# One of the last four units by Strassen's scheme instead of two, and a reordered start of the value loads

## The chip, the core and the metric

The kernel runs on one core of a Trainium2 chip. A core has TensorE (PE; its weight loads are shown apart as PEld), VectorE (DVE), ScalarE (ACT), GpSimd (POOL) and SyncE (SP), each with its own in-order stream of instructions, and 16 DMA engines that all queues share. The metric is the device time of one execution in microseconds (us); lower is better.

## The reference

Two stages. The first is attention over 8 batches of 8 heads with head dimension 64: 32 global and 512 local tokens per batch. Global queries see all 544 keys; a local query sees the 32 global keys and the local keys within 32 positions of its own.

```python
s_g = scale * np.matmul(q_g, k_all.transpose(0, 1, 3, 2))
out_g = np.matmul(sm(s_g), v_all)
s_ll = np.where(np.abs(pos[:, None] - pos[None, :]) <= window, s_ll, -1000000000.0)
a_l = sm(np.concatenate([s_lg, s_ll], axis=-1))
out_l = np.matmul(a_l, np.concatenate([v_g, v_l], axis=2))
```

The second is a mixture of 8 experts over the 4352 resulting rows x (512 wide, 1024 hidden) in which every expert is applied to every row; the weights P come from eight rounds of row and column normalisation.

```python
P = np.exp(logits - logits.max())
for _ in range(8):
    P /= P.sum(1, keepdims=True) + 1e-09
    P /= P.sum(0, keepdims=True) + 1e-09
    P *= N / E
for e in range(E):
    out += P[:, e:e + 1] * (np.maximum(x @ w1[e], 0.0) @ w2[e])
```

The output is 4352 x 512 in float32.

## The kernel before

**Order.** The instructions of each engine run in the order in which the program issues them (`manual_schedule`), so the order of the source is the order of each queue. The framework adds the semaphore waits: an instruction waits for earlier ones that touch the same region of a tile. What it takes for the same region matters here. Partitions are told apart exactly. Columns that interleave are not always: in the program of the kernel before, the first load into `va` (columns 0 to 63 of each 65) waits for the VectorE memset of the ones column (column 64 of each 65, L293), the load into `vb` waits for the memset of its ones column (L294), and the first `vgz` load waits for the POOL copy into the ones column of `vgz` (L298), though none of these pairs shares an element.

**Start.** Before the attention loop the kernel loads the first queries and keys, clears tiles and loads batch 0's values. Loads that change the type to float16 go through POOL's queue (`nc.gpsimd.dma_start`), where issuing one keeps POOL busy for 0.6 to 0.9 us; loads without a change of type go through SP or ACT.

- `steps[2:4]` load queries and keys of heads 4 to 7 of batch 0 (`qs`, `ks`, L174).
- `load_v(b)` returns the steps that load a batch's local values: `first` (L193, with the cast of the global values ahead of it, L183, by `cast_vg`), `mid` (L196, three loads) fill `va`; `last` (L200) fills a part of `vb`; `part` copies the rest of `vb` out of `va`, shifted by half a block of 128 tokens (L204 to L209, for batches 0 and 1 on POOL). 65 columns per head: 64 values and a one, so that the softmax sum comes out of the same matmul.
- `cast_vg(b)` writes the global values of a batch as float16 to a scratch in DRAM (`vg16`); `load_vz(b)` loads them from there into `vgz`, a tile of zeros with the values on a quarter of the partitions for each of four blocks (L180, four loads on SP).
- `clear(i, eng)` sets the first 32 partitions of `va` to zero (L292) and the ones columns of `va` (L293) and `vb` (L294). `clear_z(i, eng)` zeroes `vgz` (L297), writes its ones column (L298) and prepares `vgn` (L300, L301), the global values for the global queries.

**Attention loop.** Each step `s` of 34 works on one pair of heads: `st_A` transposes keys and queries (L332), `st_B` makes scores, maxima and exponentials (L368 to L382), `st_D1` and `st_D2` transpose the probabilities (L389, L399, L403), `st_E` multiplies them with the values (L423: for each block first `va` or `vb`, then `vgz`) and normalises (L427, L428). POOL's queue in step 1 is: four loads of batch 1's queries and keys, the five `vb` copies (`part`), the loads of w1 of expert 0 and of the gate; in step 2 the loads of batch 1's values. `st_E(0)` stands at the end of step 2, and PE's later work queues behind it. From step 5 on matmuls of experts 0 and 1 fill PE's idle time.

**Experts 2 to 7** run as matmuls of quarters by Strassen's scheme (Winograd's form): a `Slot` is a block of the first layer (L969), a `Unit` a block of 256 tokens of the second (L871). A unit needs four sums on its inputs (`sums`, L867) and seven products `m1` to `m7` of four matmuls of 256 columns each; they gather in one tile `z` of PSUM (two buffers) with two ACT copies inside PSUM (L885, L892), and DVE adds them to the output in `r2`, `r7` and `r1` (L905).

**The last four units** `u0` to `u3` have no slot work beside them. `plain(u, last, between)` makes a unit without the scheme: 2 x 8 matmuls of 512 columns (L940) and an addition per half (L943); `between` places other products behind a given matmul. Before: `u0` plain, `u1` and `u2` by the scheme, `u3` plain with the rest of `u2` in between; the sums of `u2` run on POOL, those of `u1` on DVE. With `last`, the second half is cut in columns of 256, 128 and 128.

Of the kernel before, what the change touches and what calls it, by code (L numbers as in the profile page):

```python
# [23 lines left out]
def kernel(  # L24
# [13 lines left out]
    nc = tc.nc  # L38
# [14 lines left out]
    FT = F // P  # L53
# [75 lines left out]
    with ExitStack() as att:  # L129
# [13 lines left out]
        vgr = [att_c.tile([P, 4 * H * VW], FP16, name=f"vgz{i}") for i in range(2)]  # L143
# [8 lines left out]
        def natural(b):  # L152
            return b < 2
# [18 lines left out]
        def load_qk(b, *hs):  # L172
            staged[b] = tuple(att_in.tile([P, H, NJ, Dh], FP16, tag=t, name=t) for t in ("qs", "ks"))
            return [lambda t=t, src=src, h0=h0, h1=h1: nc.gpsimd.dma_start(  # L174
                        out=t[:, h0:h1], in_=src[b, h0:h1].rearrange("h (p s) d -> p h s d", s=NJ))
                    for h0, h1 in zip(hs, hs[1:]) for t, src in zip(staged[b], (q_l, k_l))]

        def load_vz(b):
            for i in range(4):
                nc.sync.dma_start(out=vgz[b % 2][i:P:4, i, :, 0:Dh], in_=vg16[b])  # L180

        def cast_vg(b):
            nc.gpsimd.dma_start(out=vg16[b], in_=v_g[b].rearrange("h g d -> g h d"))  # L183

        def load_v(b):
            va, vb = vab[b % 2]
            vz = vgz[b % 2]
            src = v_l[b].rearrange("h s d -> s h d")

            def first():  # L190
                if b != 1:
                    cast_vg(b)
                nc.gpsimd.dma_start(out=va[W:P, 0, :, 0:Dh], in_=src[0:96])  # L193

            def mid(j):
                nc.gpsimd.dma_start(out=va[:, j, :, 0:Dh], in_=src[P * j - W : P * j + 96])  # L196

            def last():
                r = HB if natural(b) else W
                nc.gpsimd.dma_start(out=vb[r : r + W, NJ - 1, :, 0:Dh], in_=src[Sl - W : Sl])  # L200

            def part(eng, lo):
                if lo:
                    eng.tensor_copy(out=vb[96:P, NJ - 1], in_=va[W : 2 * W, 0])  # L204
                    eng.tensor_copy(out=vb[0:HB, 0:2], in_=va[HB:P, 0:2])
                    eng.tensor_copy(out=vb[0:HB, 2:NJ], in_=va[HB:P, 2:NJ])
                else:
                    eng.tensor_copy(out=vb[HB:P, 0:2], in_=va[0:HB, 1:3])
                    eng.tensor_copy(out=vb[HB:P, 2], in_=va[0:HB, 3])  # L209

            def move():
                if natural(b):
                    return part
                nc.sync.dma_start(out=vb[96:P, NJ - 1], in_=va[W : 2 * W, 0])
                nc.sync.dma_start(out=vb[0:W, :], in_=va[HB : HB + W, :])
                nc.sync.dma_start(out=vb[HB : HB + W, :], in_=va[HB + W : P, :])
                nc.sync.dma_start(out=vb[W:HB, 0 : NJ - 1], in_=va[0:W, 1:NJ])
                nc.sync.dma_start(out=vb[HB + W : P, 0 : NJ - 1], in_=va[W:HB, 1:NJ])
                load_vz(b)

            return [first] + [lambda j=j: mid(j) for j in range(1, NJ)] + [last, move]
# [38 lines left out]
        def run(steps):  # L260
            for f in steps:
                f()
# [14 lines left out]
        steps = load_qk(0, 2, 4, H)  # L277
# [12 lines left out]
        def clear(i, eng):  # L290
            va, vb = vab[i]
            eng.memset(va[0:W, 0], 0.0)  # L292
            eng.memset(va[:, :, :, Dh:VW], 1.0)  # L293
            eng.memset(vb[:, :, :, Dh:VW], 1.0)  # L294

        def clear_z(i, eng):
            eng.memset(vgr[i].bitcast(mybir.dt.uint32), 0)  # L297
            eng.tensor_copy(out=vgz[i][:, :, :, Dh], in_=own.unsqueeze(2).to_broadcast([P, 4, H]))  # L298
            if i == 0:
                eng.memset(vgn[0 : P - Sg], 0.0)  # L300
                eng.memset(vgn[P - Sg : P, :, Dh:VW], 1.0)  # L301

        clear(0, nc.vector)
        clear(1, nc.vector)
        for t in range(2):
            (nc.vector.tensor_copy if t else nc.scalar.copy)(out=staged[0][t][:, 0:2], in_=fh[t])
        for a in range(2):
            band = mask[HB * a : HB * (a + 1), 1, 0:KW]
            for base, m, c in ((0, -1, 1), (2 * W, 1, -1)):
                nc.gpsimd.affine_select(out=band, in_=band, compare_op=ALU.is_ge, fill=NEG, base=base,  # L310
                                        pattern=[[c, KW]], channel_multiplier=m)
        run(steps[2:4])
        *steps, move = load_v(0)
        part = move()
        run(steps)
        cast_vg(1)
        clear_z(0, nc.gpsimd)
        load_vz(0)
        nc.sync.dma_start(out=vgn[P - Sg : P, :, 0:Dh], in_=vg16[0])

        st = {}
# [248 lines left out]
        for s in range(NU + 2):  # L570
            b, hp = divmod(s, HP)
# [189 lines left out]
    with tc.tile_pool(name="tpool", bufs=2) as tpool, \  # L761
# [68 lines left out]
        def store(m, c, eng):  # L830
            if m < B:
                r0 = S * m + Sg + P * c
                eng.dma_start(out=out[r0 : r0 + P, :], in_=ogs[m][:, c, :])
            else:
                for b in range(4 * c, 4 * c + 4):
                    eng.dma_start(out=out[S * b : S * b + Sg, :], in_=ogs[m][W * (b % 4) : W * (b % 4 + 1), c, :])
# [15 lines left out]
        class Unit:  # L852
# [6 lines left out]
            def o(self, j):  # L859
                return acc_of(self.m)[:, self.c[j], :]  # L860

            def sums(self, eng=nc.vector):
                a11, a12, a21, a22 = self.a
                s = self.s = hsum.tile([P, 3, HF, P], FP16, tag="hs", name="hs")
                for o, x, y, op in ((s[:, 1], a11, a21, ALU.subtract), (a21, a21, a22, ALU.add),
                                    (s[:, 0], a21, a11, ALU.subtract), (s[:, 2], a12, s[:, 0], ALU.subtract)):
                    eng.tensor_tensor(out=o, in0=x, in1=y, op=op)  # L867

            def mm(self, o, lhs, rhs, first):
                for fk in range(HF):  # L870
# [3 lines left out]
            def w(self, i, j):  # L874
                return w2s[self.k][:, HF * i : HF * (i + 1), H2 * j : H2 * (j + 1)]
# [55 lines left out]
        def plain(u, last, between):  # L931
            order = sorted(range(FT), key=lambda fk: (fk % HF == HF - 1, fk))
            for j in range(2):
                for d0, d1 in ((0, H2), (H2, 3 * P), (3 * P, D)) if last and j else ((0, D),):
                    pool, tag = (ps_sc, "sc") if (j + (d0 > 0)) % 2 else (ps_mm, "mm")
                    z = pool.tile([P, D], FP32, tag=tag, name="zp")
                    for n, fk in enumerate(order):
                        for f in between.get((j, n), ()) if d0 == 0 else ():
                            f()
                        nc.tensor.matmul(z[:, d0:d1], u.a[2 * j + fk // HF][:, fk % HF, :], work["last"][:, fk, d0:d1],  # L940
                                         start=(n == 0), stop=(n == FT - 1), skip_group_check=True)
                    o = u.o(j)[:, d0:d1]
                    nc.vector.scalar_tensor_tensor(out=o, in0=z[:, d0:d1], scalar=u.p[j], in1=o, op0=ALU.mult, op1=ALU.add)  # L943
                store(u.m, u.c[j], nc.sync)
# [171 lines left out]
        p, x = state["slot"], state["unit"]  # L1116
        for w in (x.m4, x.m5, x.r2, x.r7, p.m4, p.m3):
            w()
        u0, u1, u2, u3 = final
        u1.sums()  # L1120
        plain(u0, False, {(0, FT - 2): (x.m3, x.r1, lambda: u2.sums(nc.gpsimd)), (1, 3): (u1.m1,)})
        for w in (u1.m7, u1.m2, u1.m6, u2.m1, u1.m4, u1.m5, u1.r2, u1.r7, u2.m7, u2.m2, u2.m6, u1.m3, u1.r1):
            w()
        plain(u3, True, {(0, 3): (u2.m4, u2.m5, u2.r2, u2.r7), (0, FT - 2): (u2.m3, u2.r1)})


# [28 lines left out]
```

## Time and profile before

| | |
|---|---|
| median of three runs | 996.98 us (996.26 to 997.41) |
| the profiled execution | 996.39 us, of which the span from the first to the last instruction is 994.6 |
| PE busy | 978.8 us, 98% of the span |
| DVE, ACT, POOL busy | 776.9, 659.8, 305.2 us |
| mean granted TensorE clock | 0.998 |

The profile shows one execution; times are in us from the start of the span. A chain of waits is followed back from the last instruction: at each step to what released it, or to the instruction before it on its engine. In a row of a timeline the first two numbers are start and length, `xN` is a number of merged instructions, and the bracket gives the idle time of the engine ahead of it and what ended it. For DMAs the row shows the issue; landing is told apart, in us from the issue.

### The profile page before, as it was taken

To read this page: it belongs to the slowest core of one execution; us is meant where nothing else is said; L and a number is where in the kernel's file an instruction comes from. 1 tells how busy PE (TensorE), PEld (TensorE's weight loads), DVE (VectorE), ACT (ScalarE), POOL (GpSimd) and SP (SyncE) were. 2 spreads that over 40 slices of the span, in tenths; PEclk is the share of its full clock that TensorE was granted. 3 is DMA by queue.
4 is the path that set the end of the run, shared out by engine and by line. 5 is a ranking of instruction groups with operands and counts; after the bars stand their busy time and mean duration, and the time that the engine had idled before them with its cause. 6 is when DMAs were issued, how large, how long until landed. Compare 5 with 4: busy or idle time off the path is not lost.

```text
span 994.6 us, 22109 instructions
## 1 busy us (share of the span) xinstructions
PE 978.8 (98%) x8644; PEld 637.0 (64%) x8644; DVE 776.9 (78%) x1919; ACT 659.8 (66%) x1372; POOL 305.2 (31%) x366
## 2 busy tenths in 40 slices
PE   7899999999999999999999999999999999999997
PEld 5565556555555556666666666676767676766765
DVE  7876666666663755899999888997899999888887
ACT  6898888888884566765555555557765555555551
POOL 9649887887860201111111111101111111100001
PEclk9999999999999999999999999999999999999999
DMA  9999999999952477554443333575654543123043
GB/s 165 189 163 207 226 213 212 224 203 234 225 141 85 121 229 189 161 138 118 117 106 75 75 74 75 138 212 138 160 138 118 117 116 71 38 56 73 2 106 128
DMA packets 138248, 138.65 MB, mean 139 GB/s; under 512 B 56800, under 2 KB 110240, under 8 KB 136096
## 3 DMA queue, kind: packets, MB, share of 16 engines
q0 software_dynamic: 105696, 87.32, 51.6%
q1 hardware_dynamic: 31888, 49.60, 15.7%
q8 instruction: 67, 1.10, 0.4%
q10 hardware_dynamic: 560, 0.33, 0.1%
q14 instruction: 37, 0.30, 0.1%
HBM read 144.46 MB, written 39.58 MB: 185 GB/s over the span
## 4 chain that ended last, share of the span: by engine, by line
PE 93%; DVE 2%; ACT 2%; POOL 1%; DMA 1%; issue 1%; SPq 0%; ACTq 0%; DVEq 0%; POOLq 0%
PE z L871 30%; PE pa L969 18%; PE py L537 12%; PE ph L523 11%; PE pb L969 9%; PE pc L969 4%; PE sc L375 1%; PE po L423 1%; PE ptw L389 1%; ACT Pu L382 1%; PE pk L332 1%; DMA vgz<-vg 1%; PE tgx L399 1%; PE pq L332 1%; PE sg L455 0%
## 5 line engine op out<-in xcount | busy, mean ns | idle before, releaser
L871 PEld LDWEIGHTS <-hs 128*128 128x128 f16 x2320 | 226.1, 98 | 96.1 <-issue 2.9
L871 PE MATMUL z<-w2e,hs 128*128 128x256 f16 x1336 | 200.4, 273 | 2.3 <-DVE o L905 1.0
L871 PE MATMUL z<-v,hs 128*128 128x256 f16 x984 | 147.6, 273 | 0.0
L892 ACT COPY z<-z 128x256 f32<-128x256 f32 x100 | 35.7, 357 | 145.9 <-PE z L871 145.9
L523 PE MATMUL ph<-xT,w1e 128*128 128x512 f16 (+1 forms) x576 | 130.2, 367 | 0.6 <-ACT xT L407 0.6
L537 PE MATMUL py<-w2e,hT 128*128 128x512 f16 x544 | 128.2, 379 | 0.0
L382 ACT ACTIVATE Pu<-ms,mx 128x160 f16<-128x160 f32 x256 | 119.6, 637 | 11.7 <-DVE mx L379 9.6
L969 PEld LDWEIGHTS <-w1e 128*128 128x128 f16 x960 | 87.1, 98 | 51.6 <-issue 1.0
L969 PE MATMUL pa<-t,s 128*128 128x512 f16 x384 | 114.2, 379 | 0.0
L787 POOL DMA_DIRECT2D w1e<-in_moe_w_dram x24 | 17.4, 733 | 290.7 <-PE pa L969 220.4
L379 DVE CUSTOM_DVE_ANT_0 ms<-sc,mask 128x160 f32<-128x160 f32 x256 | 70.0, 320 | 46.3 <-ACT yst L540 27.6
L867 DVE TENSOR_TENSOR hs<-hs 128x512 f16<-128x512 f16 x228 | 99.1, 435 | 8.4
L905 DVE SCALAR_TENSOR_TENSOR oy<-z,lg,oy 128x512 f32<-128x512 f32 x128 | 95.8, 748 | 7.3 <-ACT oy L910 5.9
L787 POOL DMA_DIRECT2D w2e<-in_moe_w_dram x24 | 19.8, 830 | 243.6 <-PE z L871 214.2
L973 DVE CUSTOM_DVE_ANT_0 hx<-pb,s 128x512 f16<-128x512 f32 x96 | 65.9, 686 | 36.4 <-ACT s L1003 30.4
L523 PEld LDWEIGHTS <-w1e 128*128 128x128 f16 x576 | 54.5, 98 | 53.0 <-issue 1.1
L989 ACT ACTIVATE hs<-pa 128x512 f16<-128x512 f32 x96 | 57.2, 596 | 46.8 <-PE pa L969 46.8
L973 DVE CUSTOM_DVE_ANT_0 hs<-pb,s 128x512 f16<-128x512 f32 x96 | 65.8, 686 | 24.1 <-ACT s L1003 23.7
L969 PEld LDWEIGHTS <-s 128*128 128x128 f16 x720 | 65.6, 98 | 28.5 <-issue 0.3
L537 PEld LDWEIGHTS <-hT 128*128 128x128 f16 x544 | 49.9, 98 | 51.9
L528 DVE TENSOR_SCALAR hT<-ph 128x512 f16<-128x512 f32 x58 | 40.1, 691 | 50.1 <-PE ph L523 50.0
L526 ACT ACTIVATE hT<-ph 128x512 f16<-128x512 f32 (+1 forms) x86 | 50.7, 589 | 27.6 <-PE ph L523 27.1
(203 smaller groups left out, 1935.0 us busy)
## 6 DMA issues: line engine op xcount, KB each, us to landing
ys<-yd SPq DMA_DIRECT2D x68, 256.0 KB, 3.2
yd<-yst SPq DMA_DIRECT2D x16, 1024.0 KB, 6.4
pw<-in_moe_w_dram POOLq DMA_DIRECT2D x24, 512.0 KB, 10.1
kept<-psum POOLq DMA_DIRECT2D x24, 512.0 KB, 4.8
s<-kept POOLq DMA_DIRECT2D x12, 768.0 KB, 8.8
v<-kept POOLq DMA_DIRECT2D x12, 768.0 KB, 8.7
w1e<-in_moe_w_dram POOLq DMA_DIRECT2D x12, 512.0 KB, 5.4
w2e<-in_moe_w_dram POOLq DMA_DIRECT2D x12, 512.0 KB, 6.5
```

The costliest lines, as they stand in the source:

```text
L379: nc.vector.tensor_tensor_reduce(out=ms[:, ii, :], in0=sc[:, SW * ii : SW * (ii + 1)], in1=mask[:, mi, :], scale=-scale, scalar=BIG, op0=A ...
L382: nc.scalar.activation(out=d["Pu"][:, i // 4, :, i % 4], in_=ms[:, ii, :], func=AF.Exp, scale=-1.0, bias=d["mx"][:, i : i + 1])
L523: nc.tensor.matmul(ph[:, 0:n], wts[e][0][:, dk, P * fm : P * (fm + 1)], xT[:, dk, c0 : c0 + n], start=(dk == 0), stop=(dk == DP - 1))
L526: nc.scalar.activation(out=hT[:, fm, 0:n], in_=ph[:, 0:n], func=AF.Relu)
L528: nc.vector.tensor_scalar(out=hT[:, fm, 0:n], in0=ph[:, 0:n], scalar1=0.0, scalar2=None, op0=ALU.max)
L537: nc.tensor.matmul(py, hT[:, fk, P * c : P * (c + 1)], wts[e][1][:, fk, :], start=(fk == 0), stop=(fk == FT - 1))
L867: eng.tensor_tensor(out=o, in0=x, in1=y, op=op)
L871: nc.tensor.matmul(o, lhs[:, fk, :], rhs[:, fk, :], start=(first and fk == 0), stop=(fk == HF - 1), skip_group_check=True)
L905: nc.vector.scalar_tensor_tensor(out=o, in0=z, scalar=p, in1=o, op0=ALU.mult, op1=ALU.add)
L969: nc.tensor.matmul(o, lhs[:, dk, P * f : P * (f + 1)], rhs[:, dk], start=(first and n == 0 and dk == 0), stop=(dk == HD - 1), skip_group_c ...
L973: nc.vector._custom_dve(TENSOR_ADD_SAT, out=self.to(i, j), in0=self.of(ps), in1=self.of(s), s0=BIG, s1=0.0)
L989: nc.scalar.activation(out=self.to(1, 0), in_=self.of(self.pa), func=AF.Relu)
```

## The change

The diff has two halves. In the end of the kernel, `u2` becomes a plain unit: its sums and products go, the rest of `u1` is placed inside `u2`'s matmuls, and `u3` follows with nothing in between. In the start, the cast of batch 0's global values is issued ahead of the loads of heads 4 to 7; the zeros of `vgz` 0 are written by VectorE where it used to do `clear(0)` and `clear(1)`; the ones of `vgz` 0 and the preparation of `vgn` follow the first load of `va`; the four `vgz` loads are issued on SP ahead of the cast of batch 1; and both `clear` calls move to POOL, behind all loads of batch 0's values.

```diff
--- before.py
+++ after.py
@@ -188,7 +188,7 @@
             src = v_l[b].rearrange("h s d -> s h d")
 
             def first():
-                if b != 1:
+                if b > 1:
                     cast_vg(b)
                 nc.gpsimd.dma_start(out=va[W:P, 0, :, 0:Dh], in_=src[0:96])
 
@@ -294,14 +294,14 @@
             eng.memset(vb[:, :, :, Dh:VW], 1.0)
 
         def clear_z(i, eng):
-            eng.memset(vgr[i].bitcast(mybir.dt.uint32), 0)
+            if i:
+                eng.memset(vgr[i].bitcast(mybir.dt.uint32), 0)
             eng.tensor_copy(out=vgz[i][:, :, :, Dh], in_=own.unsqueeze(2).to_broadcast([P, 4, H]))
             if i == 0:
                 eng.memset(vgn[0 : P - Sg], 0.0)
                 eng.memset(vgn[P - Sg : P, :, Dh:VW], 1.0)
 
-        clear(0, nc.vector)
-        clear(1, nc.vector)
+        nc.vector.memset(vgr[0].bitcast(mybir.dt.uint32), 0)
         for t in range(2):
             (nc.vector.tensor_copy if t else nc.scalar.copy)(out=staged[0][t][:, 0:2], in_=fh[t])
         for a in range(2):
@@ -309,13 +309,17 @@
             for base, m, c in ((0, -1, 1), (2 * W, 1, -1)):
                 nc.gpsimd.affine_select(out=band, in_=band, compare_op=ALU.is_ge, fill=NEG, base=base,
                                         pattern=[[c, KW]], channel_multiplier=m)
+        cast_vg(0)
         run(steps[2:4])
         *steps, move = load_v(0)
         part = move()
-        run(steps)
+        steps[0]()
+        clear_z(0, nc.gpsimd)
+        run(steps[1:])
+        load_vz(0)
         cast_vg(1)
-        clear_z(0, nc.gpsimd)
-        load_vz(0)
+        clear(0, nc.gpsimd)
+        clear(1, nc.gpsimd)
         nc.sync.dma_start(out=vgn[P - Sg : P, :, 0:Dh], in_=vg16[0])
 
         st = {}
@@ -859,12 +863,12 @@
             def o(self, j):
                 return acc_of(self.m)[:, self.c[j], :]
 
-            def sums(self, eng=nc.vector):
+            def sums(self):
                 a11, a12, a21, a22 = self.a
                 s = self.s = hsum.tile([P, 3, HF, P], FP16, tag="hs", name="hs")
                 for o, x, y, op in ((s[:, 1], a11, a21, ALU.subtract), (a21, a21, a22, ALU.add),
                                     (s[:, 0], a21, a11, ALU.subtract), (s[:, 2], a12, s[:, 0], ALU.subtract)):
-                    eng.tensor_tensor(out=o, in0=x, in1=y, op=op)
+                    nc.vector.tensor_tensor(out=o, in0=x, in1=y, op=op)
 
             def mm(self, o, lhs, rhs, first):
                 for fk in range(HF):
@@ -1118,10 +1122,11 @@
             w()
         u0, u1, u2, u3 = final
         u1.sums()
-        plain(u0, False, {(0, FT - 2): (x.m3, x.r1, lambda: u2.sums(nc.gpsimd)), (1, 3): (u1.m1,)})
-        for w in (u1.m7, u1.m2, u1.m6, u2.m1, u1.m4, u1.m5, u1.r2, u1.r7, u2.m7, u2.m2, u2.m6, u1.m3, u1.r1):
+        plain(u0, False, {(0, FT - 2): (x.m3, x.r1), (1, 3): (u1.m1,)})
+        for w in (u1.m7, u1.m2, u1.m6):
             w()
-        plain(u3, True, {(0, 3): (u2.m4, u2.m5, u2.r2, u2.r7), (0, FT - 2): (u2.m3, u2.r1)})
+        plain(u2, False, {(0, 3): (u1.m4, u1.m5, u1.r2, u1.r7), (1, 3): (u1.m3, u1.r1)})
+        plain(u3, True, {})
 
 
 # ---- launch: one core; inputs and outputs as the reference has them ----
```

## The prediction

> **What bounds the kernel now.** I read the page's busy times first, then the busy times by stretch, then the chain of waits of the first 80 us, the timelines of POOL and of the last 35 us, and the DMA queues' own waits.
>
> ```profile
> PE 978.8 (98%) x8644; PEld 637.0 (64%) x8644; DVE 776.9 (78%) x1919; ACT 659.8 (66%) x1372; POOL 305.2 (31%) x366
> ```
>
> PE is the bound, and it lacks only 994.6 - 978.8 = 15.8 us. The stretches tell where those are:
>
> ```profile
> 0.00:50.00 50.00, 40.32 (x745) 27.07 (x746) 40.58 (x185) 39.93 (x91) 40.53 (x63) 0.97 1.52 177
> ...
> 970.00:994.60 24.60, 19.02 (x142) 13.05 (x140) 17.85 (x27) 3.91 (x9) 4.79 (x4) 0.99 0.34 129
> ```
>
> The columns after the length are PE, PEld, DVE, ACT and POOL busy, the granted clock, DMA share and GB/s. 9.7 us of PE's idle time lie in the first 50 us and 5.6 in the last 24.6; between them PE is full, so whatever delays the front arrives undiminished at the end. Both halves of the change sit at these ends. The front's chain of waits:
>
> ```profile
> 13.96 0.61 SPq L180
> 14.61 6.71 DMA vgz<-vg
> 21.36 0.53 PE po L423 x21
> ```
>
> Columns are start, length, what. Ahead of these the chain runs along POOL's queue. The last vgz transfer lands at 21.32, and PE, which had begun step 2's values (`st_E(0)`) at 20.35, waits 0.64 us for it; DVE then sits idle 0.78 us before the reciprocal at 21.91. From there the chain goes through DVE and ACT until about 58 us, with no DMA in it. What else could hold `st_E(0)` is on POOL:
>
> ```profile
> 5.86 0.66 POOL L183 DMA_DIRECT2D vg<-in_v_g_dram  x1
> ...
> 16.20 0.61 POOL L204 COPY vb<-va 32x520 f16<-32x520 f16 x1
> ...
> 18.97 1.05 POOL L208 COPY vb<-va 64x1040 f16<-64x1040 f16 x1
> 19.96 0.61 POOL L209 COPY vb<-va 64x520 f16<-64x520 f16 x1
> ```
>
> `st_E(0)` reads vb from its second matmul on, and vb is whole only at 20.58. The vgz wait has 0.8 us of cover to give back, and right under it lies the end of POOL's queue.
>
> **Change 1, the end.** From 974.9 PE runs plain u0, Strassen u1 and u2, plain u3.
>
> ```profile
> 976.49 4.45 DVE L867 TENSOR_TENSOR hs<-hs 128x512 f16<-128x512 f16 x4
> ...
> 981.66 0.60 PE L871 MATMUL z<-w2e,hs 128*128 128x256 f16 x4 [0.97 <-DVE oy L905]
> ...
> 988.51 0.60 PE L871 MATMUL z<-w2e,hs 128*128 128x256 f16 x4 [0.98 <-DVE o L905]
> ...
> 988.94 2.36 PE L940 MATMUL zp<-w2e,hs 128*128 128x512 f16 x26
> ```
>
> u1's four sums take 4.45 us on DVE beside u2's four on POOL (5.02 us); the four of the unit before took 0.42 each, 1.7 together. That delays `x.r1` to 980.87, for which `u2.m1` waits 0.97. A further 0.32 (984.76) and 0.98 (988.51) pass in front of u2's m4 and m3, which follow their readers too closely. The change removes u2's sums and all three waits: 2.27 us. It swaps 7 x 4 matmuls of 256 columns (0.109 us start to start, 3.05) for 16 of 512 (0.217, 3.47): +0.42. By this sum the gain is 1.85.
>
> Laying out the new order gives more. u1's m6 ends its issue at 980.53. Then come 16 matmuls of u2 (3.47), u1's m4, m5 and m3 (12 x 0.109 = 1.30) and u3 (8 x 0.217, 8 x 0.109, 16 x 0.054 = 3.47): 988.8 plus a 0.2 drain, against 991.3 before: -2.3. The difference is time lost around u2's scattered groups, which the waits do not list. New waits: m4 needs the z copy of ACT (980.73 to 981.09 before) and arrives at 981.18; m3 at 983.8 needs r2's read, due at 983.0. Both are covered, by 0.1 and 0.8 us. The finish behind PE (3.3 us of DVE, store and landing) stays. I take **-2.3**, bounds -2.6 and -1.8.
>
> **Change 2, the front.** POOL loses the vgz memset (0.96), DVE takes it. The cast of vg 0 goes ahead of the qs and ks loads, 1.5 us earlier. vgz's ones and vgn follow va's first load; SP can then issue the vgz loads as soon as vg has landed, about 9 us (qs, which takes its place in the queue, landed at 10.1) instead of 12.65. That removes the vgz wait: at most the 0.78 us of DVE.
>
> Against it POOL gets both `clear`s, behind all of va 0's loads. By length one costs 0.61 (the vgn memset, 520 elements as well) plus two of some 0.15, two cost 1.8; less the 0.96, POOL's queue grows by 0.8 and vb with it: 21.4. Without any wait this eats the gain: front 0.0.
>
> But the clears do wait. The second memset of `clear(0)` writes va's ones column, in a tile whose other columns the four va loads are filling, and the third one vb's, beside the vb load. The framework treats such interleaved columns as overlapping:
>
> ```profile
> SPq L180 <- POOL vgz L298: 10.2, 1, 10.2
> ```
>
> This is a row of the DMA queues' waits: the first vgz load (columns 0 to 63) started at 12.65, behind the POOL copy into column 64 that ended at 12.62, although vg had landed at 12.47 and the memset ended at 12.23. The program of before says the same for the very tiles: the first va load waits for the VectorE memset of va's ones, the vb load for that of vb's. With the order reversed, POOL's memsets wait for the loads' landing, and POOL works in order: queued behind them are batch 1's four qs and ks loads, the vb copies, w1e and batch 1's va.
>
> ```profile
> vb<-in_v_l_dram POOLq DMA_DIRECT2D x1, 32.0 KB, 6.4
> ```
>
> Issued at 9.90, vb landed 6.4 us later, at 16.3. Now vgz and vgn (160 KB) go ahead of much of it; va's 128 KB loads land 1.1 us apart, so this adds 0 to 1.4, I take 1.0: 17.3. Then the rest of the clears 1.0, four loads 3.05 (13.15 to 16.20 before), five copies 4.38 (16.20 to 20.58): vb is whole at 25.75 instead of 20.58. PE stops in front of `st_E(0)`'s second matmul from 20.35 until L208's end at 25.2, and finishes half of its matmuls (0.27) and a drain of 0.2 behind L209, at 26.2 instead of 21.9: **+4.3**, bounds 3.3 (vb at 16.3) and 4.8 (vb at 17.8). DVE and ACT have nothing else: their next instructions wait for `st_E(0)` or for what PE has queued behind it. Later users have cover: batch 1's qs and ks, issued from 18.3, are wanted at 29; w1e at 43; vb 1's copies end near 42.7 for use at 44.8.
>
> A stop of 4.9 us also touches the clock:
>
> ```profile
> 8.00:12.00 4.00, 2.12 (x40) 1.61 (x36) 3.55 (x20) 3.88 (x10) 3.96 (x6) 0.87 1.77 176
> 12.00:16.00 4.00, 4.00 (x71) 2.70 (x69) 3.16 (x14) 3.12 (x8) 3.88 (x8) 0.70 2.46 128
> ```
>
> After a stretch with PE half idle the granted clock fell (0.87, then 0.70), and eight ptw transposes took 1.04 us instead of 0.64. I add one such batch on the path: **+0.4**, bounds 0 and 1.0.
>
> The Trainium skill (TensorE: Matmul & The Clock Gate, Part 1: The HAM clock gate) says that one idle window of about 3.4 us halves the clock until a busy window has passed; by that the price would be up to half a window, an estimate of 1.7 us, and the sum 3.7 instead of 2.4. The dip in the row above came without such a long stop.
>
> **Sum.** -2.3 + 4.3 + 0.4 = +2.4; bounds +0.7 (-2.6 + 3.3) and +4.0 (-1.8 + 4.8 + 1.0). The profiled execution took 996.39 (span 994.6), 0.6 below the median of 996.98; set on the median: **999.4**. A measurement of this kernel can tell about 0.2%, 2.0 us, from no change; the forecast lies just past that.
>
> **Rivals.**
> - *The clears don't wait* (faster, 0.10): the overlap rule might count only in the old direction. Then POOL is 0.8 later, the front gives 0.0 and the end -2.3: 994.7. It decides at vb: whole by 21.4. Against it stand both waits of the program before.
> - *A shorter stop* (same, 0.25): vb lands at 16.3 to 16.8 because vgz queues behind va, and the clock holds: front 3.3 to 4.0, sum +0.7 to +2.0, 998.3.
> - *The end gives nothing* (slower, 0.07): u1's m4 and m3 inside u2 wait as u2's did inside u3, and only +0.42 of matmuls is left: 996.98 + 4.7 + 0.4 = 1002.1. DVE without the POOL sums speaks against it.
>
> My forecast, a sum from +2.0 to +4.0, has 0.58. Slower is this and the third rival, 0.65. The range from 997.6 to 1001.2 takes in the second rival and leaves out the first and the third.
>
> **What would show it.** POOL's timeline: L293 starting near 17 behind an idle stretch of some 4 us with va's load as releaser, L204 at 21 to 22, L209 ending near 25.8; PE idle about 5 us before L423, and the clock below 1 near 24 to 28. In the end: u1's sums at 0.42 each, no PE wait on L905, last matmul about 2.3 us closer to its start at 974.9. L204 near 17 would prove me wrong in the front, PE waits in u2's matmuls in the end.

## The result and the profile after

The changed kernel takes 1000.86 us (median of 6 executions, 999.38 to 1002.8) against 996.81 for the kernel before in the same comparison: ratio 1.004 (95% interval 1.0027 to 1.0053), slower by 0.4%. The profiled execution took 1000.84 with a span of 999.0, 4.4 longer than before's 994.6. Code below the edits has moved down by four lines: before's L423 (`po`) is L427, L867 and L871 (sums and products of the scheme) are L871 and L875, L905 is L909, L940 and L943 (plain units) are L944 and L947.

The page of the changed kernel, busy times:

```profile
PE 981.9 (98%) x8632; PEld 637.5 (64%) x8632; DVE 772.9 (77%) x1913; ACT 659.4 (66%) x1370; POOL 301.0 (30%) x367
```

PE's idle time is 999.0 - 981.9 = 17.1 us, 1.3 more than before; the rest of the 4.4 is busy time, with 12 matmuls fewer, and the clock is at half for 10.2 us of the first 50 where it was for 3.4. The stretches of the same trace (columns as before: PE, PEld, DVE, ACT, POOL busy, granted clock, DMA share, GB/s) show that the front has lost and the end has won. The last stretch starts with u0's first matmul.

```profile
0.00:50.00 50.00, 36.97 (x634) 24.66 (x634) 34.07 (x154) 33.73 (x76) 40.51 (x67) 0.90 1.30 149
24.00:28.00 4.00, 1.07 (x31) 0.98 (x30) 0.00 (x0) 0.00 (x0) 3.94 (x5) 0.84 1.28 161
28.00:32.00 4.00, 4.00 (x91) 3.38 (x89) 3.65 (x16) 2.31 (x5) 4.00 (x6) 0.73 0.88 133
981.60:999.00 17.40, 14.13 (x97) 8.69 (x95) 10.78 (x19) 0.96 (x3) 0.00 (x0) 1.00 0.39 151
```

In the first 50 us PE has 36.97 us of work where it had 40.32, and 634 matmuls where it had 745. From 24 to 28 only POOL is at work: PE stands still for most of it, DVE and ACT for all of it. Then the granted clock is at half, from 26.71 to 30.13, and eight `ptw` transposes that took 0.64 us before (at 22.17) take 1.04 (at 28.62). POOL's timeline shows what it is doing meanwhile, and what it did before that:

```profile
12.11 0.52 POOL L292 MEMSET va<- 32x520 f16 x1
18.91 0.25 POOL L293 MEMSET va<- 128x32 f16 x1 [6.28 <-DMA va<-in_v_l_dram]
19.01 0.28 POOL L294 MEMSET vb<- 128x32 f16 x1
...
23.06 0.61 POOL L204 COPY vb<-va 32x520 f16<-32x520 f16 x1
...
25.83 1.05 POOL L208 COPY vb<-va 64x1040 f16<-64x1040 f16 x1
26.83 0.62 POOL L209 COPY vb<-va 64x520 f16<-64x520 f16 x1
```

The first memset of `clear(0)` runs at once. The second, 32 columns of ones that lie between the columns that the loads fill, stops POOL for 6.28 us until the last `va` load has landed, at 18.81; the third, on `vb`, then waits until 18.97. Everything else then comes in POOL's order: the rest of the clears, four loads from 20.01, five copies. `vb` is whole at 27.45 instead of 20.58. PE's waits in the first 80 us, and then the chain of waits:

```profile
PE po L427 <- POOL vb L208: 5.1, 1, 5.1
```

```profile
9.87 8.94 DMA va<-in_v_l_dram
...
25.83 1.06 POOL vb L208
26.93 1.17 PE po L427 x30
```

Before, the chain went through the last `vgz` transfer and PE waited 0.64 us. Now the `vgz` loads are in no row of PE's waits, and in their place stands a `va` load of 8.94 us with POOL's whole queue behind it. The loads of batch 0's local values land late (the DMA issues, last column from issue to landing):

```profile
va<-in_v_l_dram POOLq DMA_DIRECT2D x1, 128.0 KB, 8.9
...
vb<-in_v_l_dram POOLq DMA_DIRECT2D x1, 32.0 KB, 8.2
```

The last `va` load is issued at 9.87 and lands at 18.81 (before: 9.04 and 16.02). `vb` is issued at 10.74 and lands at 18.97. Before, it was issued at 9.90, took 6.4 and landed at 16.3: now it starts 0.84 later and takes 1.8 longer. The end, from DVE's timeline and then PE's:

```profile
983.21 1.87 DVE L871 TENSOR_TENSOR hs<-hs 128x512 f16<-128x512 f16 x4
```

```profile
981.61 1.46 PE L944 MATMUL zp<-w2e,hs 128*128 128x512 f16 x6
...
988.77 1.89 PE L944 MATMUL zp<-w2e,hs 128*128 128x512 f16 x8
990.56 0.60 PE L875 MATMUL z<-w2e,hs 128*128 128x256 f16 x4
991.00 4.74 PE L944 MATMUL zp<-w2e,hs 128*128 128x512 f16 x37
```

u1's four sums are back to 1.87 us from 4.45, and among PE's waits behind 970 us there is no row left. From u0's first matmul to PE's end it is 14.12 us (981.61 to 995.73) where it was 16.40 (974.90 to 991.30): 2.28 gained. The same marker says what the front cost: u0 starts 6.71 later. 6.71 - 2.28 = 4.43, which is the difference of the spans.

### The profile page after: what moved, and what is told of

Read it like the earlier page. It is cut to its first block, busy times and chain, and to the rows that moved or that the text cites. A ratio compares the mean times of both kernels' runs of the same rounds, so it can differ in the third digit from the quotient of the medians.

```text
span 999.0 us, 22075 instructions
## 1 busy us (share of the span) xinstructions
PE 981.9 (98%) x8632; PEld 637.5 (64%) x8632; DVE 772.9 (77%) x1913; ACT 659.4 (66%) x1370; POOL 301.0 (30%) x367
## 4 chain that ended last, share of the span: by engine, by line
PE 94%; ACT 2%; POOL 1%; DVE 1%; DMA 1%; issue 0%; POOLq 0%; ACTq 0%; DVEq 0%
PE z L875 30%; PE pa L973 18%; PE py L541 12%; PE ph L527 11%; PE pb L973 9%; PE pc L973 4%; PE po L427 1%; PE ptw L393 1%; PE sc L379 1%; PE zp L944 1%; ACT Pu L386 1%; DMA va<-in_v_l_dram 1%; PE pk L336 1%; PE tgx L403 1%; PE pq L336 1%
## 5 line engine op out<-in xcount | busy, mean ns | idle before, releaser
L875 PEld LDWEIGHTS <-hs 128*128 128x128 f16 x2292 | 223.3, 98 | 93.4 <-DVE hs L871 1.5
L875 PE MATMUL z<-w2e,hs 128*128 128x256 f16 x1320 | 198.0, 273 | 0.0
L875 PE MATMUL z<-v,hs 128*128 128x256 f16 x972 | 145.8, 273 | 0.0
L791 POOL DMA_DIRECT2D w1e<-in_moe_w_dram x24 | 17.4, 733 | 290.9 <-PE pa L973 220.6
L871 DVE TENSOR_TENSOR hs<-hs 128x512 f16<-128x512 f16 x228 | 96.6, 423 | 8.7 <-DVE hs L871 0.5
L909 DVE SCALAR_TENSOR_TENSOR oy<-z,lg,oy 128x512 f32<-128x512 f32 x128 | 95.8, 749 | 7.3 <-ACT oy L914 5.9
```

The costliest lines, as they stand in the source:

```text
L871: nc.vector.tensor_tensor(out=o, in0=x, in1=y, op=op)
L875: nc.tensor.matmul(o, lhs[:, fk, :], rhs[:, fk, :], start=(first and fk == 0), stop=(fk == HF - 1), skip_group_check=True)
L909: nc.vector.scalar_tensor_tensor(out=o, in0=z, scalar=p, in1=o, op0=ALU.mult, op1=ALU.add)
```

## The experiments

My theory was the prediction's: the ones columns of `clear(0)` wait for the loads into the same tiles, POOL's queue behind them makes `vb` late, and this is the whole loss; the end gains 2.3 on its own. The rivals: the loss comes from the later landing of `vb` and `va` itself, whatever POOL does meanwhile; or from the clock; or the two halves act on each other. Ratios are to the kernel before, run beside each experiment; each line of measurements gives the median, then the ratio with its 95% interval.

**One half alone.** `front_only` is the changed kernel with before's end (`sums` with its engine argument, u2 by the scheme); `end_only` is the kernel before with the changed end.

> The front of the change with the end of before. If the two halves simply add, the front alone costs what the changed kernel lost plus what its end gave back: 4.4 us of span plus 2.3, so 6.7 us over before, some 1003.5. Theory 'the clears wait for the landings': in POOL's timeline L293 of the first clear starts behind an idle stretch of 5 to 7 us and vb is whole near 27.4. Rival 'the halves act on each other' (the loads of the last experts, or the shift itself, change the end): a loss off 6.7 by more than 1 us.

Measured: 1002.65, 1.0053 (1.004 to 1.0065). PE waits 5.5 us for L208; u0 starts at 981.38, 6.48 late, and the end takes 16.41, as before.

> The end of the change with the front of before. If the halves add: 2.3 us faster than before, 994.5, with the first L93x/L94x matmul of u0 at the same time as before (974.9) and the span ending 17.4 us behind it instead of 19.7. Rival 'the end's gain was only the place of the stop': within 0.5 us of before.

Measured: 994.96, 0.998 (0.997 to 0.999). The end takes 14.12, as in the changed kernel. The time of `front_only` is 5.1 us over the kernel before beside it, 1.6 less than I expected, a sign of the rival by the letter of the expectation. Most of the 1.6 lies in what I counted from: one profile of the kernel before, 996.39, whose median beside this run is 997.56. The ratios multiply to 1.0033, against 1.004 for the whole: the times agree with halves that add, to about 2 us, which is what their intervals resolve. The traces speak against the rival: the old end takes 16.41 behind the new front and 16.40 behind the old one, the new end 14.12 behind either, so neither half changes the other. The clock in `front_only` was another matter. Its stretches:

```profile
24.00:28.00 4.00, 2.04 (x47) 1.83 (x47) 0.80 (x2) 0.00 (x0) 3.94 (x6) 0.56 1.12 140
28.00:32.00 4.00, 4.00 (x78) 3.32 (x75) 3.20 (x17) 2.62 (x6) 3.96 (x6) 0.59 1.01 166
```

The clock is halved from 24.46 to 31.29, 6.83 us, twice as long as in the changed kernel's profile (26.71 to 30.13). From the first reciprocal behind `st_E(0)` to the third it takes 7.28 us, against 6.25 before: 1.03 for the clock.

**The clears moved out of the loads' way.** In `clears_first` POOL does them ahead of `va`'s first load; all else is the changed kernel, and POOL's work is the same.

```diff
+        clear(0, nc.gpsimd)
+        clear(1, nc.gpsimd)
         steps[0]()
         clear_z(0, nc.gpsimd)
 ...
         cast_vg(1)
-        clear(0, nc.gpsimd)
-        clear(1, nc.gpsimd)
```

> The whole change, but both clears stand on POOL ahead of va's first load instead of behind all of batch 0's loads: the same work on the same queue in another place. Theory 'the clears wait for the landings': no idle stretch on POOL, vb whole about 0.8 us later than before (21.4), st_E(0) held by it for at most a microsecond, and the time at 994.5 to 995.5. Rival 'POOL simply has too much work': the work is the same, so the loss stays, 1000 to 1001. Rival 'the early cast and the vgz loads crowd the DMA queue': they stay too, so most of the loss stays, over 999.

Measured: 994.96, 0.9975 (0.9965 to 0.9985). POOL's timeline:

```profile
7.38 0.24 POOL L293 MEMSET va<- 128x32 f16 x1
...
20.78 0.61 POOL L209 COPY vb<-va 64x520 f16<-64x520 f16 x1
```

No idle time stands before any memset, `vb` is whole at 21.39, and PE has no wait for POOL. The `vb` load lands at 18.4 here, later than in `front_only` (18.0), and it holds nothing up: L204 has started at 17.01, with the four loads of batch 1 issued before it. So the late landing alone is not the loss. It is the wait placed ahead of POOL's other work.

In `clear0_vector` only `clear(0)` goes back to VectorE, early, behind the `vgr` memset; `clear(1)` stays late on POOL.

```diff
         nc.vector.memset(vgr[0].bitcast(mybir.dt.uint32), 0)
+        clear(0, nc.vector)
 ...
-        clear(0, nc.gpsimd)
         clear(1, nc.gpsimd)
```

> The whole change, but clear(0) stays on VectorE ahead of the loads; clear(1), whose tiles nothing is loading yet, stays late on POOL. Theory 'the clears wait for the landings': only clear(0) met loads in flight, so the stop goes: POOL has 0.96 us of vgz memset less and about 0.9 of clear(1) more than before, vb is whole near 20.6, vgz has landed earlier, st_E(0) ends up to 0.8 us earlier than before: 993.8 to 994.8, faster than both kernels. Rival 'POOL simply has too much work': half of the clears' work is left, so about half of the loss, 998.

Measured: 994.50, 0.9969 (0.9958 to 0.998). The first reciprocal comes at 21.45, 0.46 earlier than before, and `vb` is whole at 20.94. (That 0.46 is one profile's: `end_all_plain` below has the same front, and there it comes at 21.82.) Of `clear`'s two calls only that on the tiles being loaded does harm. `ones_early` goes one step further: VectorE writes only batch 0's ones columns early, and the first memset of `clear(0)`, on other rows of `va`, stays behind the loads on POOL (L323 in its listing).

```diff
         nc.vector.memset(vgr[0].bitcast(mybir.dt.uint32), 0)
+        for t in vab[0]:
+            nc.vector.memset(t[:, :, :, Dh:VW], 1.0)
 ...
-        clear(0, nc.gpsimd)
+        nc.gpsimd.memset(vab[0][0][0:W, 0], 0.0)
         clear(1, nc.gpsimd)
```

> The whole change, but the two memsets of batch 0's ones columns go back to VectorE ahead of the loads; the memset of va's first 32 partitions (L292) and all of clear(1) stay late on POOL. (Those 32 rows of the ones column then stay zero; they belong to masked positions, whose probability is zero.) Theory 'only the interleaved columns are taken for the loads' region': L292 writes partitions that no load writes, so it does not wait, the stop goes, 994 to 995.5. Rival 'any late write into a tile that is being loaded waits': L292 waits for va's landing near 18 and the time stays at 1000 to 1001.

Measured: 994.50, 0.9976 (0.9966 to 0.9985). POOL's timeline:

```profile
12.13 0.52 POOL L323 MEMSET va<- 32x520 f16 x1
...
20.24 0.62 POOL L209 COPY vb<-va 64x520 f16<-64x520 f16 x1
```

The memset on rows that no load touches starts at once, with the loads under way. What waits is the write into columns that lie between the loads' columns.

**Does the early cast crowd the loads?** `cast_late` puts batch 0's `cast_vg` back behind the loads of heads 4 to 7, so that the `vgz` loads start later; the clears stay late.

```diff
-        cast_vg(0)
         run(steps[2:4])
+        cast_vg(0)
```

> The whole change, but the cast of vg 0 stands behind the qs and ks loads again, so SP can issue the vgz loads only near 12.5 and they queue behind va. Theory 'the size of the stop is the landing of vb, and the early vgz loads crowd it': vb lands at 16.3 to 17.3 instead of 19.0, L293 starts then, vb is whole near 25.5 and the time is 1.5 to 2.5 us under the changed kernel, 998.5 to 999.5. Rival 'vb's late landing is a straggling DMA engine that has nothing to do with the order': vb lands at 18 to 19 and the time stays at 1000 to 1001.

Measured: 999.67, 1.0025 (1.0013 to 1.0038); PE waits 4.2 us. POOL's timeline:

```profile
16.39 0.25 POOL L293 MEMSET va<- 128x32 f16 x1 [3.76 <-DMA va<-in_v_l_dram]
17.71 0.25 POOL L294 MEMSET vb<- 128x32 f16 x1 [1.07 <-DMA vb<-in_v_l_dram]
```

`va` and `vb` now land 1.36 us apart, at 16.30 and 17.66, and the two memsets wait one after the other, each for its own tile. I expected `vb` at 16.3 to 17.3; the time came out above my range, and its interval overlaps that of the whole change. So the earlier `vgz` loads do not explain the late landing by themselves, and the traces of all runs show what else goes into it. First, `vb` is issued at 10.72 here too and not at 9.90: the `vgz` ones and `vgn`'s memsets now stand on POOL between `va`'s first load and the rest. Second, the same load varies from run to run: from issue to landing it took 6.4, 7.2 and 7.8 us in three profiles with the front of before (the kernel before, `end_only`, `end_sums_vector`), 6.9 in `cast_late`, and 6.7 to 8.2 in eight with the early cast behind the same queue. `va`'s last load, for which the first memset waits, took 7.0 to 8.5 with the front of before, 6.4 in `cast_late`, and 7.3 to 8.9 with the early cast. A share for crowding can't be told from this spread and one profile of `cast_late`; it stays open.

**The clock.** `filled_stop` is the changed kernel with fourteen filler matmuls of 128x512 on PE ahead of `st_E(0)` in step 2, so that PE isn't idle in the stop.

```diff
             if s == 2:
+                keep_busy(14)
                 st_E(0)
```

> The whole change with 14 matmuls of 512 columns, whose results nothing reads, in front of st_E(0) in PE's queue (some 3.0 us at full clock): they fill the stop without lengthening it. Theory 'the stop also costs clock': no half-clock window behind the stop, the two reciprocals of step 2 and 3 stand 2.2 us apart as before instead of 2.41, and the time is 0.2 to 1.0 us lower. Rival 'the clock costs nothing here, since DVE and ACT set the pace': the same 2.4 us between the reciprocals and no difference in time.

Measured: 999.47, 1.0024 (1.0013 to 1.0035). The granted clock stays at 1 and the wait on PE shrinks to 1.2. Since the time hangs on a landing that scatters, the same kernel and the changed kernel were run again, side by side.

> The changed kernel, unaltered, beside the next run on one chip. Its first profile had vb landing at 18.97; the other kernels with the early cast had it at 17.9 to 18.4. Theory: that one was a straggler and this one lands near 18.0, so the time is 999.5 to 1000.5, 3 to 3.5 over before.

Measured: 1000.47, 1.0038 (1.0024 to 1.0052).

> The stop filled with 14 matmuls as above. If the clock behind the stop costs one half-clock window, 0.2 to 0.3 us under the unaltered changed kernel; if mostly two windows, as in the profile of the front alone, about 1.0 under it; if the lower time of the first comparison was vb's landing and not the clock, no difference.

Measured: 999.75, 1.0034 (1.0021 to 1.0047). Its stretches:

```profile
24.00:28.00 4.00, 3.36 (x88) 2.31 (x86) 1.57 (x9) 0.40 (x1) 3.94 (x6) 1.00 0.99 127
28.00:32.00 4.00, 3.03 (x62) 2.13 (x58) 2.80 (x12) 3.73 (x10) 3.96 (x6) 1.00 1.06 183
```

The times do not separate filled from unfilled: 0.7 us lies between the medians of the second pair, less than the intervals, and the profile of `filled_again` loses 1.1 us later in one wait for a `vgz` landing. The profiles do separate them. `changed_again` and `filled_stop` happen to agree on `vb` (landed at 17.96 in both, whole at 26.40 and 26.39), and behind it the clock differs. From the first reciprocal to the third the one takes 7.33 us, with half clock from 24.49 to 31.32, and the other 6.24, as before (6.25): 1.09 for the clock. u0 then starts at 981.41 in the one and at 980.27 in the other.

**What the end consists of.** `end_sums_vector` is the kernel before with u2's sums on VectorE instead of POOL.

```diff
-        plain(u0, False, {(0, FT - 2): (x.m3, x.r1, lambda: u2.sums(nc.gpsimd)), (1, 3): (u1.m1,)})
+        plain(u0, False, {(0, FT - 2): (x.m3, x.r1, lambda: u2.sums()), (1, 3): (u1.m1,)})
```

> The kernel before with one edit: u2's four sums on VectorE instead of POOL, in the same place of the program. It splits the gain of the end. Theory 'of the 2.3 us, 1.0 is u1's sums slowed by POOL's, the rest is u2's products that follow their readers too closely': u1's sums take 1.7 instead of 4.45, the wait of 0.97 at u2.m1 goes, those of 0.3 and 1.0 at u2's m4 and m3 stay, the first L940 matmul to the end takes 18.7 instead of 19.7 us, 996. Rival 'the products' order is all of it': no gain. Rival 'the slow sums are all of it': 2 us or more of gain, 995 or less.

Measured: 996.23, 0.9993 (0.9983 to 1.0002): the time can't be told from before's. PE's waits behind 960 us:

```profile
PE z L871 <- DVE o L905: 1.0, 1, 1.0
PE z L871 <- DVE ox L905: 0.3, 1, 0.3
```

The wait of `u2.m1` (0.97 before) is gone, the other two are still there. They are not both u2's, as my prediction had it: by the order of the source the 0.32 stands in front of u1's m3, and only the 0.98 in front of u2's m3. u1's sums take 1.87 us, and the end 15.45 where before took 16.40: 0.95 of the gain was POOL's sums slowing DVE's, and the other 15.45 - 14.12 = 1.33 is the order of the products around u2's. A row of waits shows less than it costs, because it counts from the end of the matmul ahead, and matmuls overlap. In the kernel before:

```profile
980.10 0.60 PE L871 MATMUL z<-v,hs 128*128 128x256 f16 x4
981.66 0.60 PE L871 MATMUL z<-w2e,hs 128*128 128x256 f16 x4 [0.97 <-DVE oy L905]
```

Four matmuls at 0.109 us start to start would bring the next one at 980.53; it starts at 981.66, 1.13 later, where the row says 0.97. In the same way the 0.32 costs 0.48 and the 0.98 costs 1.14. In `end_sums_vector` those two and 0.17 in front of `u2.m1`, which no row names, less the 0.42 that 512-column matmuls cost more, give 1.37, near the 1.33.

`end_all_plain` is `clear0_vector` with u1 plain as well, so no unit of the four by the scheme.

```diff
-        u1.sums()
-        plain(u0, False, {(0, FT - 2): (x.m3, x.r1), (1, 3): (u1.m1,)})
-        for w in (u1.m7, u1.m2, u1.m6):
-            w()
-        plain(u2, False, {(0, 3): (u1.m4, u1.m5, u1.r2, u1.r7), (1, 3): (u1.m3, u1.r1)})
+        plain(u0, False, {(0, FT - 2): (x.m3, x.r1)})
+        plain(u1, False, {})
+        plain(u2, False, {})
         plain(u3, True, {})
```

> The kernel with clear(0) on VectorE and, on top, u1 plain as well, so that all of the last four units are plain. Taking u2 out of the scheme paid because its sums and its products' order cost more than the 0.42 us of matmuls saved. For u1 nothing waits any more: theory 'the scheme pays where its waits are covered': 0.4 us slower than with u1 by the scheme (first L944 matmul to the last PE end 14.5 instead of 14.1), some 995. Rival 'plain is better throughout, since the scheme's groups of four cost PE time that no wait shows': equal or faster.

Measured: 994.68, 0.9978 (0.9969 to 0.9987). The end takes 14.45, 0.33 more than with u1 by the scheme, and the times of the two do not differ measurably. By the traces one unit by the scheme is worth a third of a microsecond here; the second one, as the kernel before had it, cost 2.3.

The version to keep is `clear0_vector` or `ones_early`: the changed end, the early cast, and batch 0's ones written before its loads. Both beat both kernels, with upper ends of 0.998 and 0.9985. That they beat `end_only` (0.997 to 0.999) is not shown: the intervals overlap. So the reordered start is not shown to give anything, even without the wait: the first reciprocal comes at 21.45 in `clear0_vector`, but at 22.12 in `ones_early` and 22.34 in `clears_first`, against 21.91 before.

## Why the prediction was right, and where it was off

**The sign and its cause.** The clears do wait, POOL's order passes the wait on, and PE stops at L208. `clears_first`, `clear0_vector` and `ones_early` each take away the wait, the first with the same work on the same queue, and each makes the slower kernel a faster one. The rival in which the clears don't wait priced such a kernel at 994.7; they took 994.96, 994.50 and 994.50.

**The stop: +4.3 predicted, +6.2 measured** (first reciprocal at 28.14, not 26.2). This is the mis-sized term, outside its bounds of 3.3 to 4.8, and most of it is one input: `vb`'s landing, taken as 17.3 (16.3 plus 1.0 for crowding), was 18.97, above even the upper bound of 17.8. The sum also left out `va`: its last load landed at 18.81, so that with an early `vb` the stop would have been hardly shorter. Two things are in the late `vb`. The issue comes 0.84 later, because `clear_z`'s ones and the `vgn` memsets were moved on POOL ahead of three of `va`'s loads and of `vb`'s; I had named that move and charged nothing for it to the loads behind it. And the 6.4 us from issue to landing were one profile's value read as exact, where the front of before alone gives 6.4 to 7.8. With 0.84 and the middle of these, 7.2, `vb` lands at 17.9, which is what `front_only`, `changed_again` and `filled_stop` show (18.0, 17.96, 17.96); the last microsecond of the 18.97 is in none of these. The chain behind the landing was right to a tenth: L204 started 4.09 behind it (1.0 + 3.05 predicted), and `vb` was whole 8.48 behind it (8.45 predicted). The last 0.2 is that the matmuls behind L209 ran at half clock, with 0.69 us from its end to the reciprocal where I had taken 0.47.

**The clock: +0.4 predicted, 0.24 measured in this profile** (6.49 us from the first reciprocal to the third, 6.25 before), 1.03 and 1.09 in `front_only` and `changed_again`. `cast_late`, behind a stop of 4.2 us, has 0.41. The bounds of 0 to 1.0 nearly held. The estimate of 1.7 from the Trainium skill was reached in none of the four.

**The end: -2.3 predicted, -2.28 measured.** Laying out the new order gave it. The simple sum, waits removed less matmuls added, gave 1.85; the prediction put the rest down to time lost around u2's groups. It is in the three waits themselves, which cost 1.13, 0.48 and 1.14 start to start, 2.75 and not the 2.27 listed; less 0.42 for the matmuls that is 2.33, near the 2.28 measured. One step of the layout was wrong, and it was luck that it cost nothing: u1's m3 was said to need only the read of `r2`, with 0.8 us to spare. It comes behind `r7` (DVE's timeline of the changed kernel):

```profile
988.97 1.54 DVE L909 SCALAR_TENSOR_TENSOR ox<-z,lg,ox 128x512 f32<-128x512 f32 x2 [1.91 <-PE z L875]
```

This row, `r2` and `r7` of u1, ends at 990.51, and m3 starts at 990.56, where the eight matmuls from 988.77 on would have let it start at 990.50. In the kernel before it was the same: `r2` and `r7` ended at 984.71, and m3 started at 984.76. A slightly later `r7` would have been a wait. The rival in which the end gives nothing is refuted by `end_only`.

**The total.** 6.23 for the stop, 0.24 for the clock and 0.24 more before u0 starts, less 2.28, is 4.43 in the profile, against +2.4. The time of 1000.86 lies in the range and 1.5 above the forecast. That it does is partly luck: the stop passed its upper bound by 1.4 and the sum its own of +4.0, and the time stayed inside because the clock cost less than forecast, the end gave what was forecast, and the range reached 0.2 beyond 996.98 + 4.0. Two small slips in the sums change nothing: `vb` at 16.3 + 1.4 is 17.7, and a `vb` at 16.8 gives a stop of 3.8, not 4.0. The rival of the shorter stop needed `vb` by 16.8, and in no profile with the early cast did it land before 17.4.

## What to carry to other kernels

Before moving a write behind a load on an in-order queue, ask whether the two touch the same tile in columns that interleave: the write then waits for the landing, and its price is not its own 0.25 us but everything issued behind it. Put constants into a tile ahead of the loads that fill the rest of it. Run the halves of a change apart as well: here a gain of 2.3 us was hidden under a loss of 6 that moving one call undoes. And measure a wait on PE from start to start, since the listed idle time leaves out the overlap that was lost.

## What the runs showed of the hardware

**The price of a lowered clock depends on where its window falls.** Stops of 5.1 to 5.5 us in front of the same code were followed by one stretch of half clock of 3.41 us or by one of 6.83, for 0.24 or 1.03 to 1.09 us. The Trainium skill (TensorE: Matmul & The Clock Gate, Part 1: The HAM clock gate) says that the activity window is about 3.4 us long and free-running, so that the point of the change varies between runs. The traces agree: the stretches behind the stop measure 3.4 or 6.8 us, and they start anywhere from 24.46 to 26.71. The profiles of `end_only`, `clear0_vector` and `end_sums_vector`, two of them with the front of before, also have 3.4 us of half clock between 31.7 and 35.7, with no wait of PE for POOL ahead of it, where before and `clears_first` have none. By the first `py` matmul it cost them 1.2 us (32.47 behind the third reciprocal in `clear0_vector`, 31.24 before). In such a profile a kernel that is faster at the first reciprocal is later at u0: `clear0_vector` starts u0 at 975.83, before at 974.90.

The stretch of half clock ahead of the stop varies too. It lasts 3.41 us in the kernel before, `front_only`, `clear0_vector` and `changed_again`, where `st_E(0)` starts at 20.20 to 20.36; it lasts 6.83 in the other profiles without fillers, where `st_E(0)` starts at 20.77 to 21.61. The changed kernel shows both, 21.61 in its first profile and 20.32 in `changed_again`. No run sets this stretch at will, so that it is the cause is read from these rows and not tried; it would also account for the later first reciprocals of `ones_early` and `clears_first`.

**A landing is set by its slowest part.** The trace has 16 completions for each of these loads. In the changed kernel's profile 15 of the last `va` load's have come by 16.92 and 15 of `vb`'s by 17.29; the sixteenth of each comes at 18.81 and 18.97, 1.9 and 1.7 us later. Meanwhile, from 16 to 18.8, POOL's DMA queue moved only 76 packets, at 5.8% of 16 engines, and started none between 16.41 and 17.25. What held the last part back is not shown.

**POOL and DVE on the same kind of operation.** Four sums of 128x512 in fp16 take 1.87 us on DVE alone and 4.45 beside four on POOL. The Trainium skill (SBUF — State Buffer, Who interferes with whom) says that a `tensor_tensor` with both inputs in SBUF contends with GpSimd's reads. `end_sums_vector` agrees: with the POOL sums gone, the same four take 1.87.
